# A two-stage Fourier transform beside attention, paired score matmuls and squares on GpSimd

## The chip, the cores and the metric

The kernel runs on one core of one Trainium2 chip. The metric is the device time of that core in microseconds (us); the time quoted for a kernel is the median of its runs.

The engines are called as in the profile: PE is TensorE (its weight loads are PEld), DVE is VectorE, ACT is ScalarE, POOL is GpSimd, SP is the engine that only issues DMA here. "L211" is line 211 of the kernel's source. An eviction is the copy of a matmul's result out of its PSUM tile (the memory that PE writes, here `ps`) into SBUF, the memory that the other work reads; ACT or DVE makes it.

## The reference

Attention without softmax makes `x` from `u`, `v` and `z`. Then `x` is projected three ways, the middle projection is convolved along the sequence with a filter by Fourier transforms, and two gates and an output projection follow. There are 8 batches, 3136 positions (64 times 49) and 256 channels; `z` has 64 channels.

```python
scores = z @ z.T / S                      # S = 3136
attn   = np.maximum(scores, 0.0) ** 2
x      = u * (attn @ v)

x1, x2, x3 = split(x @ w_proj)            # 3 x 256 channels
conv = irfft(rfft(x2) * rfft(filter_fft)) # along S
out  = (x1 * conv * x3) @ w_out
```

## The kernel before

It is two programs one after the other. The first does attention and the projections, and builds sine and cosine tables of 3136 by 1569 on the side; the second does the transform as matrix products with these tables, forward and back.

Attention, for a chunk of 512 queries and one block of 128 keys:

```python
ps = psA_sc.tile([P, CH], F32, name="ps_sc")
nc.tensor.matmul(ps[:krows, :cw], zT16[:, ds(kt * P, krows)], zT16[:, ds(s0, cw)], ...)   # L211, 64 rows
nc.scalar.activation(R[:krows, :cw], ps[:krows, :cw], AF.Relu)                            # L214
if kt % ACT_SQUARE_EVERY == (ACT_SQUARE_EVERY - 1):
    nc.scalar.activation(A16[...], R[...], AF.Square)
else:
    nc.vector.tensor_tensor(A16[...], R[...], R[...], ALU.mult)
for dh in range(2):
    nc.tensor.matmul(psout[:, dh, :cw], v16[:, kt, ds(dh * P, P)], A16[:, kt, :cw], ...)  # L222, 128 rows
```

The dense transform, forward (cosine and sine for every frequency block `ft`), then inverse:

```python
for t in range(NST):                                  # 25 blocks of positions
    for cN in range(NCH2):
        nc.tensor.matmul(pacc[:fw, 0, cN, :cwN], bandc[...], x2h[...], ...)     # L338
        nc.tensor.matmul(pacc[:fw, 1, cN, :cwN], bands[...], x2h[...], ...)     # L340
# ... product with the transformed filter, cut ...
for ft in range(NFT):                                 # 13 blocks of frequencies
    nc.tensor.matmul(po[:, :cw], Ac16[...], itC[...], start=(ft == 0), stop=False)   # L397
    nc.tensor.matmul(po[:, :cw], As16[...], itS[...], ...)                           # L399
```

Of the kernel before, what the change touches and what calls it, by code (L numbers as in the profile page):

```python
# [12 lines left out]
P = 128  # L13
# [6 lines left out]
CH = 512  # L20
ACT_SQUARE_EVERY = 4
# [3 lines left out]
def kernel(  # L25
# [14 lines left out]
    assert moe_w_proj.shape[1] == 3 * D and D == 2 * P and B % 2 == 0 and S % 4 == 0  # L40

    Fq = S // 2 + 1
    NST = ceil(S / P)
    NFT = ceil(Fq / P)
    NC = ceil(S / CH)

    def st_rows(t):
        return min(P, S - t * P)

    def ft_rows(t):  # L50
        return min(P, Fq - t * P)

    dram = ctx.enter_context(tc.tile_pool(name="dram_scratch", bufs=1, space=bass.MemoryType.DRAM))
    const = ctx.enter_context(tc.tile_pool(name="const", bufs=1))

    x2all = dram.tile([S, B * D], BF16, name="x2all")
    x1T_d = dram.tile([B * D, S], BF16, name="x1T_d")
    x3T_d = dram.tile([B * D, S], BF16, name="x3T_d")
    tabC = dram.tile([S, Fq], BF16, name="tabC")
    tabS = dram.tile([S, Fq], BF16, name="tabS")  # L60
    tabCi = dram.tile([Fq, S], BF16, name="tabCi")
    tabSi = dram.tile([Fq, S], BF16, name="tabSi")

    ident_f32 = const.tile([P, P], F32, name="ident_f32")
    make_identity(nc, ident_f32[:])
    ident_bf = const.tile([P, P], BF16, name="ident_bf")
    nc.vector.tensor_copy(ident_bf[:], ident_f32[:])
    negpi = const.tile([P, 1], F32, name="negpi")
    nc.vector.memset(negpi[:], -float(np.pi))

    wp16 = const.tile([P, 2, 3 * D], BF16, name="wp16")
# [4 lines left out]
    with ExitStack() as pha:  # L76
        tgencol = pha.enter_context(tc.tile_pool(name="tgencol", bufs=1))
        tgen = pha.enter_context(tc.tile_pool(name="tgen", bufs=2))
        batchp = pha.enter_context(tc.tile_pool(name="batchp", bufs=2))
        vpool = pha.enter_context(tc.tile_pool(name="vpool", bufs=2))  # L80
        batchin = pha.enter_context(tc.tile_pool(name="batchin", bufs=1))
        io = pha.enter_context(tc.tile_pool(name="io", bufs=2))
        achunk = pha.enter_context(tc.tile_pool(name="achunk", bufs=2))
        rring = pha.enter_context(tc.tile_pool(name="rring", bufs=4))
        ev = pha.enter_context(tc.tile_pool(name="ev", bufs=2))
        psA_pr = pha.enter_context(tc.tile_pool(name="psA_pr", bufs=2, space=bass.MemoryType.PSUM))
        psA_sc = pha.enter_context(tc.tile_pool(name="psA_sc", bufs=2, space=bass.MemoryType.PSUM))
        psA_out = pha.enter_context(tc.tile_pool(name="psA_out", bufs=1, space=bass.MemoryType.PSUM))
        tpsum = pha.enter_context(tc.tile_pool(name="tpsum", bufs=2, space=bass.MemoryType.PSUM))

        col_i = tgencol.tile([P, CH], I32, name="col_ramp_i")
        nc.gpsimd.iota(col_i[:], pattern=[[1, CH]], base=0, channel_multiplier=0)
        col_f = tgencol.tile([P, CH], F32, name="col_ramp_f")
        nc.vector.tensor_copy(col_f[:], col_i[:])
        pidx_i = tgencol.tile([P, 1], I32, name="pidx_i")
        nc.gpsimd.iota(pidx_i[:], pattern=[[0, 1]], base=0, channel_multiplier=1)
        pidx_f = tgencol.tile([P, 1], F32, name="pidx_f")
        nc.vector.tensor_copy(pidx_f[:], pidx_i[:])

        RND = float(1.5 * 2 ** 23)  # L100
        SHIFT_S = S // 2
        SHIFT_C = 3 * (S // 4)

        def table_gen_slices():
            for t in range(NST):
                rows = st_rows(t)

                def gen_band(t=t, rows=rows):
                    bandC = tgen.tile([P, Fq], BF16, name="bandC")
                    bandS = tgen.tile([P, Fq], BF16, name="bandS")  # L110
                    rowv = tgencol.tile([P, 1], F32, name="rowv")
                    nc.vector.tensor_single_scalar(rowv[:rows], pidx_f[:rows], float(t * P), ALU.add)
                    c0 = 0
                    while c0 < Fq:
                        w = min(CH, Fq - c0)
                        kf = tgencol.tile([P, CH], F32, name="kf")
                        if c0 == 0:
                            nc.vector.tensor_scalar(kf[:rows, :w], col_f[:rows, :w],
                                                    rowv[:rows, 0:1], None, ALU.mult)
                        else:  # L120
                            cf2 = tgencol.tile([P, CH], F32, name="cf2")
                            nc.vector.tensor_single_scalar(cf2[:rows, :w], col_f[:rows, :w], float(c0), ALU.add)
                            nc.vector.tensor_scalar(kf[:rows, :w], cf2[:rows, :w],
                                                    rowv[:rows, 0:1], None, ALU.mult)
                        t1 = tgencol.tile([P, CH], F32, name="t1")
                        nc.vector.tensor_scalar(t1[:rows, :w], kf[:rows, :w], 1.0 / S, RND, ALU.mult, ALU.add)
                        q0 = tgencol.tile([P, CH], F32, name="q0")
                        nc.vector.tensor_single_scalar(q0[:rows, :w], t1[:rows, :w], RND, ALU.subtract)
                        r = tgencol.tile([P, CH], F32, name="r")
                        nc.vector.scalar_tensor_tensor(r[:rows, :w], q0[:rows, :w], -float(S), kf[:rows, :w],  # L130
                                                       ALU.mult, ALU.add)
                        mneg = tgencol.tile([P, CH], F32, name="mneg")
                        nc.vector.tensor_single_scalar(mneg[:rows, :w], r[:rows, :w], 0.0, ALU.is_lt)
                        u1 = tgencol.tile([P, CH], F32, name="u1")
                        nc.vector.scalar_tensor_tensor(u1[:rows, :w], mneg[:rows, :w], float(S), r[:rows, :w],
                                                       ALU.mult, ALU.add)
                        for shift, band in ((SHIFT_S, bandS), (SHIFT_C, bandC)):
                            m2 = tgencol.tile([P, CH], F32, name="m2")
                            nc.vector.tensor_single_scalar(m2[:rows, :w], u1[:rows, :w], float(S - shift), ALU.is_ge)
                            up = tgencol.tile([P, CH], F32, name="up")  # L140
                            nc.vector.tensor_single_scalar(up[:rows, :w], u1[:rows, :w], float(shift), ALU.add)
                            uu = tgencol.tile([P, CH], F32, name="uu")
                            nc.vector.scalar_tensor_tensor(uu[:rows, :w], m2[:rows, :w], -float(S), up[:rows, :w],  # L143
                                                           ALU.mult, ALU.add)
                            nc.scalar.activation(band[:rows, ds(c0, w)], uu[:rows, :w], AF.Sin,
                                                 bias=negpi[:rows], scale=2.0 * np.pi / S)
                        c0 += w
                    nc.sync.dma_start(out=tabC[ds(t * P, rows), :], in_=bandC[:rows, :])
                    nc.sync.dma_start(out=tabS[ds(t * P, rows), :], in_=bandS[:rows, :])

                yield gen_band

        tslices = table_gen_slices()

        def emit_table_slices(n):
            for _ in range(n):
                fn = next(tslices, None)
                if fn is None:
                    return False
                fn()  # L160
            return True

        total_slices = NST
        slices_per_chunk = max(1, ceil(total_slices / max(1, B * NC)))

        inv_s2 = 1.0 / float(S) ** 2

        def batch_setup(b):
            zT16 = batchp.tile([dqk, S], BF16, name="zT16")
            uT16 = batchp.tile([P, 2, S], BF16, name="uT16")  # L170
            v16 = vpool.tile([P, NST, D], BF16, name="v16")
            NSTF = S // P
            zin = batchin.tile([P, NST, dqk], F32, name="zin")
# [23 lines left out]
        for b in range(B):  # L197
            zT16, uT16, v16 = setup
            if b + 1 < B:
                setup = batch_setup(b + 1)  # L200
# [249 lines left out]
```

## Time and profile before

| | |
|---|---|
| time, median of three runs | 3166.74 us |
| attention and projections | 0 to about 1620 us |
| dense transform | about 1620 to 3176 us |
| PE busy | 2727.0 us, 86% |
| GpSimd busy | 32.0 us, 1% |

The page of the profile starts with the busy time of each engine, then shows the span in 40 equal slices: each digit is the busy share in tenths, and PEclk is the clock that PE was granted, in tenths of full speed.

```profile
span 3175.6 us, 38107 instructions
PE 2727.0 (86%) x12632; PEld 1110.5 (35%) x12860; DVE 1634.2 (51%) x3711; ACT 1328.3 (42%) x3166; POOL 32.0 (1%) x51
...
PE   5876776876879898999995999999999588889999
...
PEclk9987877886889799999897999999999799899999
```

The busy times by stretch put numbers on the two halves. The columns are: the stretch, its length, busy time and instructions of PE, PEld, DVE, ACT and POOL, the granted clock, the DMA share and GB/s.

```profile
0.00:1620.00 1620.00, 1333.29 (x5313) 450.70 (x5410) 1221.78 (x2794) 1120.08 (x2554) 18.67 (x26) 0.87 0.24 64
1620.00:3176.00 1556.00, 1393.74 (x7321) 659.80 (x7450) 412.44 (x918) 208.19 (x614) 13.29 (x25) 0.96 0.41 107
```

In the second half PE is busy 1394 of 1556 us while DVE and ACT have little to do. In the first half three engines share the load and none is full.

The timeline of PE shows when runs of matmuls start (first column, us). Inside a run a 128x512 matmul starts every 0.215 us: three take 0.81 us and one alone takes about 0.38.

```profile
1573.82 0.81 PE L222 MATMUL psoutT<-A_16476,v_14198 128*128 128x512 bf16 x3
1574.56 0.39 PE L211 MATMUL ps_sc<-zT_14196 64*128 64x512 bf16 x1
1574.88 0.61 PE L222 MATMUL psoutT<-A_16476,v_14198 128*128 128x512 bf16 x2
```

From the score matmul (64 rows) to the next value matmul (128 rows) it is 0.32 us, not 0.215: about 0.1 us is lost at the change.

### The profile page before, as it was taken

To read this page: it belongs to the slowest core of one execution; us is meant where nothing else is said; L and a number is where in the kernel's file an instruction comes from. 1 tells how busy PE (TensorE), PEld (TensorE's weight loads), DVE (VectorE), ACT (ScalarE), POOL (GpSimd) and SP (SyncE) were. 2 spreads that over 40 slices of the span, in tenths; PEclk is the share of its full clock that TensorE was granted. 3 is DMA by queue.
4 is the path that set the end of the run, shared out by engine and by line. 5 is a ranking of instruction groups with operands and counts; after the bars stand their busy time and mean duration, and the time that the engine had idled before them with its cause. 6 is when DMAs were issued, how large, how long until landed. Compare 5 with 4: busy or idle time off the path is not lost.

```text
span 3175.6 us, 38107 instructions
## 1 busy us (share of the span) xinstructions
PE 2727.0 (86%) x12632; PEld 1110.5 (35%) x12860; DVE 1634.2 (51%) x3711; ACT 1328.3 (42%) x3166; POOL 32.0 (1%) x51
## 2 busy tenths in 40 slices
PE   5876776876879898999995999999999588889999
PEld 2323222222223233333332555553444233334444
DVE  5998998898985465666661434332111122231111
ACT  4866665765777576777771112120111000001111
POOL 0000000000000000000001000000000000000000
PEclk9987877886889799999897999999999799899999
DMA  7312312212212222121017434415452633334443
GB/s 153 101 46 53 100 41 62 91 46 67 90 44 43 80 52 71 35 48 32 30 39 173 107 90 97 108 45 175 124 161 82 159 64 61 62 78 133 151 130 82
DMA packets 456118, 270.55 MB, mean 85 GB/s; under 512 B 249430, under 2 KB 440238, under 8 KB 455920
## 3 DMA queue, kind: packets, MB, share of 16 engines
q1 hardware_dynamic: 268280, 175.17, 19.0%
q10 hardware_dynamic: 158216, 77.96, 9.5%
q0 software_dynamic: 29424, 14.98, 3.5%
q8 instruction: 100, 1.64, 0.2%
q14 instruction: 98, 0.80, 0.1%
HBM read 179.32 MB, written 103.59 MB: 89 GB/s over the span
## 4 chain that ended last, share of the span: by engine, by line
PE 70%; DVE 11%; DMA 10%; ACT 5%; issue 3%; SPq 0%; ACTq 0%; DVEq 0%
PE psoutT L222 17%; PE ps_sc L211 10%; PE psB_fwd L338 9%; PE psB_fwd L340 9%; PE psB_inv L397 8%; PE psB_inv L399 8%; ACT Rblk L214 3%; DMA uin<-in_u_dram 2%; DMA itS<-tabSi 2%; PE ps_pr L192 2%; DVE uu L143 2%; DMA x1T_d<-xiT 2%; PE ps_pr L234 2%; DMA bands<-tabS 2%; PE psB_tr L321 2%
## 5 line engine op out<-in xcount | busy, mean ns | idle before, releaser
L214 ACT ACTIVATE Rblk<-ps_sc 128x512 f32<-128x512 f32 (+2 forms) x1400 | 717.5, 542 | 209.4 <-PE ps_sc L211 174.3
L338 PE MATMUL psB_fwd<-x2h,bandc 128*128 128x512 bf16 (+2 forms) x1284 | 496.7, 387 | 68.8 <-DVE As_25282 L350 33.2
L340 PE MATMUL psB_fwd<-x2h,bands 128*128 128x512 bf16 (+2 forms) x1244 | 479.7, 386 | 0.7
L416 ACT ACTIVATE ostage<-psB_out 128x256 f32<-128x256 f32 (+1 forms) x200 | 76.6, 383 | 590.6 <-PE psB_out L414 404.1
L399 PE MATMUL psB_inv<-itS,As_25282 128*128 128x512 bf16 (+3 forms) x722 | 245.8, 357 | 3.3 <-DMA itS<-tabSi 1.7
L399 PE MATMUL psB_inv<-itS,As_17634 128*128 128x512 bf16 (+3 forms) x722 | 244.4, 355 | 1.8 <-issue 0.8
L397 PE MATMUL psB_inv<-itC,Ac_17633 128*128 128x512 bf16 (+2 forms) x706 | 238.9, 355 | 5.0 <-DMA itC<-tabCi 4.6
L397 PE MATMUL psB_inv<-itC,Ac_25281 128*128 128x512 bf16 (+2 forms) x706 | 240.3, 357 | 2.6 <-DMA itC<-tabCi 2.1
L338 PEld LDWEIGHTS <-bandc 128*128 128x128 bf16 (+2 forms) x1300 | 128.5, 99 | 157.0 <-issue 54.0
L340 PEld LDWEIGHTS <-bands 128*128 128x128 bf16 (+2 forms) x1300 | 128.6, 99 | 149.1 <-issue 40.5
L322 DVE COPY inv_st_c<-psB_tr 128x128 bf16<-128x128 bf16 (+2 forms) x190 | 42.0, 221 | 252.9 <-PE psB_tr L321 218.3
L350 DVE CAST As_25282<-psB_fwd 128x512 bf16<-128x512 f32 (+1 forms) x26 | 18.0, 691 | 279.2 <-ACT Ac_25281 L349 279.2
L349 ACT ACTIVATE Ac_25281<-psB_fwd 128x512 bf16<-128x512 f32 (+1 forms) x26 | 15.5, 596 | 349.3 <-PE psB_fwd L340 339.4
L192 PE MATMUL ps_pr<-ident_f_67,uin 128*128 128x128 f32 (+1 forms) x400 | 117.3, 318 | 40.1 <-DMA uin<-in_u_dram 10.9
L247 PE MATMUL ps_pr<-wp_76,xTch 128*128 128x256 bf16 (+1 forms) x400 | 78.1, 292 | 70.5 <-ACT xiT L238 55.4
L349 ACT ACTIVATE Ac_17633<-psB_fwd 128x512 bf16<-128x512 f32 (+1 forms) x26 | 15.5, 597 | 288.9 <-PE psB_fwd L340 288.2
L234 PE MATMUL ps_pr<-xTch,wp_76 128*128 128x512 bf16 (+1 forms) x430 | 117.2, 364 | 6.0 <-ACT xiT L238 1.7
L240 DVE CAST xiT<-ps_pr 128x512 bf16<-128x512 f32 (+1 forms) x112 | 69.7, 623 | 72.3 <-DMA x1T_d<-xiT 62.4
L321 PE MATMUL psB_tr<-ident_bf,bandc 128*128 128x128 bf16 (+3 forms) x325 | 71.2, 219 | 41.2 <-DMA bandc<-tabC 31.0
L397 PEld LDWEIGHTS <-Ac_25281 128*128 128x128 bf16 (+1 forms) x728 | 68.2, 98 | 90.8 <-issue 36.3
L250 ACT ACTIVATE x2blk<-ps_pr 128x256 bf16<-128x256 f32 (+1 forms) x200 | 75.6, 383 | 58.2 <-PE ps_pr L247 32.2
L397 PEld LDWEIGHTS <-Ac_17633 128*128 128x128 bf16 (+1 forms) x728 | 67.8, 98 | 88.0 <-issue 32.9
(1891 smaller groups left out, 4695.0 us busy)
## 6 DMA issues: line engine op xcount, KB each, us to landing
uin<-in_u_dram ACTq DMA_DIRECT2D x8, 3072.0 KB
out_dram<-ostage SPq DMA_DIRECT2D x192, 128.0 KB
bands<-tabS ACTq DMA_DIRECT2D x576, 32.0 KB
bandc<-tabC SPq DMA_DIRECT2D x576, 32.0 KB
itC<-tabCi SPq DMA_DIRECT2D x144, 128.0 KB
itS<-tabSi ACTq DMA_DIRECT2D x144, 128.0 KB
x1T_d<-xiT SPq DMA_DIRECT2D x96, 128.0 KB
x3T_d<-xiT SPq DMA_DIRECT2D x96, 128.0 KB
```

The costliest lines, as they stand in the source:

```text
L192: nc.tensor.transpose(ptu[:, :rows], uin[:rows, t, ds(dh * P, P)], ident_f32[:rows, :rows])
L211: nc.tensor.matmul(ps[:krows, :cw], zT16[:, ds(kt * P, krows)], zT16[:, ds(s0, cw)], start=True, stop=True)
L214: nc.scalar.activation(R[:krows, :cw], ps[:krows, :cw], AF.Relu)
L222: nc.tensor.matmul(psout[:, dh, :cw], v16[:, kt, ds(dh * P, P)], A16[:, kt, :cw], start=(kt == 0), stop=(kt == NST - 1))
L234: nc.tensor.matmul(pp[:, :cw], wp16[:, ksub, ds((comp * 2 + nb) * P, P)], xT[:, ksub, :cw], start=(ksub == 0), stop=(ksub == 1))
L247: nc.tensor.matmul(pp[:sw, :D], xT[:, ksub, ds(sb * P, sw)], wp16[:, ksub, D:2 * D], start=(ksub == 0), stop=(ksub == 1))
L321: nc.tensor.transpose(pti[:fw, :rows], src[:rows, t, :fw], ident_bf[:rows, :rows])
L338: nc.tensor.matmul(pacc[:fw, 0, cN, :cwN], bandc[:rows, t, :fw], x2h[:rows, t, ds(cN * CH, cwN)], start=(t == 0), stop=(t == NST - 1))
L340: nc.tensor.matmul(pacc[:fw, 1, cN, :cwN], bands[:rows, t, :fw], x2h[:rows, t, ds(cN * CH, cwN)], start=(t == 0), stop=(t == NST - 1))
L397: nc.tensor.matmul(po[:, :cw], Ac16[:fw, ft, ds(col0, P)], itC[:fw, ft, :cw], start=(ft == 0), stop=False)
L399: nc.tensor.matmul(po[:, :cw], As16[:fw, ft, ds(col0, P)], itS[:fw, ft, :cw], start=False, stop=(ft == NFT - 1))
L416: nc.scalar.activation(ost[:sw, sb, :], pp[:sw, :], AF.Copy)
```

## The change

Its intent is to shrink the transform and to hide it. It has four parts.

1. The 3136 points are split as 64 by 49, so that the transform is two small matrix products with a twiddle (a phase factor, here folded into a table) between them, forward and back. Two batches are packed as the real and imaginary part of one signal.
2. These stages are cut into small units and put between the attention steps of the next two batches. Only the last pair of batches is left for the end.
3. Score matmuls go in pairs: one block of keys from partitions 0-63, the next from 64-127, where a second copy of `z` stands. One wide eviction of up to 128x1024 serves both.
4. Squares go to ACT, DVE or GpSimd, whichever has the least estimated load; evictions go to ACT or DVE in the same way.

The diff does one thing more: `u` and `z` are loaded as bf16 and not as fp32, and so are transposed as bf16.

```diff
-ACT_SQUARE_EVERY = 4
+N1 = 64
+N2 = 49
+CHUNKS = (4, 4, 4, 3, 3, 3, 4)
+LAG = 3
...
+    def scores(b, c, i):
+        ps = ps_tile()                                   # one of three PSUM tiles [P, 2, 512]
+        for j in range(2):
+            hs = ds(N1 * j, N1)
+            nc.tensor.matmul(ps[:, j, :cw], zT[hs, ds((2 * i + j) * P, P)], zT[hs, ds(s0, cw)],
+                             start=True, stop=True)                                        # L465
... the last 64 keys, which have no partner, and the views Rv, pv and Av cut ...
+        R = rring.tile([P, 2, 512], F32, name="R")       # three buffers
+        if load.take(k * cw, ("act", "dve")) == "act":
+            nc.scalar.activation(Rv, pv, AF.Relu)                                          # L474
+        else:
+            nc.vector.tensor_single_scalar(Rv, pv, 0.0, ALU.max)                           # L476
+        eng = load.take(k * cw, ("act", "dve", "pool"))
+        if eng == "act":
+            nc.scalar.activation(Av, Rv, AF.Square)                                        # L481
+        else:
+            (nc.vector if eng == "dve" else nc.gpsimd).tensor_tensor(Av, Rv, Rv, ALU.mult) # L483
... values (L496), xT (L506), projections (L421, L447) and sine tables cut ...
+    def stage1(srcs, y, t0, n): ...      # 64-point transform, evicted to ye, stored to y_d
+    def stage2(p, kb): ...               # loads yl and hl; 49-point transform (L347); product tt (L351)
+    def stage3(p, kb): ...               # 49-point inverse (L360), evicted to ve, stored to v_d
+    def stage4(p, t0, n): ...            # loads vl and gl; 64-point inverse (L384), gates (L388)
+    def stage5(p, t0, n): ...            # output projection (L404), evicted to ot, stored (L411)
...
+        own += [lambda: proj1(b, c), lambda: proj3(b, c), lambda: proj2(b, c)]
+        own.insert(min(2, len(own)), lambda: (load_u(b1, c1), tr_u(b1, c1)))
... the units in `far` are spread between these and between the steps ...
```

## The prediction

> # Prediction
>
> **What bounds the kernel before.** The busy times by stretch show attention from 0 to about 1620 us, then the dense transform of 3136 points to 3176 us. In the second stretch PE is busy 1393 of 1556 us; the timeline shows 128x512 matmuls starting every 0.215 us, and the instruction order has 3.0 M moving columns there (1254 us at 0.42 ns a column): PE-bound. In the first, PE is busy 1334 of 1620 us at a granted clock of 0.78 to 0.95; ACT evicts every score tile (596 ns for 128x512), DVE squares three quarters (690 ns) and builds sine tables. The chain of waits puts 70% on PE.
>
> **PE after.** By the order of instructions, moving columns fall from 5.25 M to 2.76 M: the dense transform's 3.0 M become about 0.6 M, and attention stays. The paired scores (0.60 M columns) sit in partitions 0-63 and 64-127; the Trainium skill, "TensorE: Matmul & The Clock Gate", Part 3, says such row tiles run at the same time. No trace here shows it yet. If so, 0.30 M more go: about 1030 us at 0.42 ns. Changing between 64-row scores and 128-row values costs about 0.1 us each way (starts 0.31 to 0.33 us apart instead of 0.215 in the timeline near 1575 us); 728 steps instead of 1400 make it 146 us, not 280. Some 1000 matmuls of 128 columns add 30 us. PE sum: about 1200 us at full clock.
>
> **The other engines** (0.157 us + columns/0.96 on DVE, 0.17 us + columns/1.2 on ACT, fitted to 690 and 596 ns): DVE about 920 us (856 k columns, all-bf16 at double rate), ACT 840 us. GpSimd was 1% busy; now it squares 335 k columns. Estimate from the Trainium skill, "GPSIMD Engine Reference", 3.1 (4497 ns for 2048 fp32): 740 us, plus 245 DMA issues at 0.57 us (140 us), plus contention with DVE: 900 to 1150 us. No trace yet shows a GpSimd square. DMA falls from 270 to about 205 MB and is hidden.
>
> **Critical path.** The stages that ran alone (1556 us) now fill gaps beside attention, so nearly all their time is won, except the last pair of batches: 71 units alone at the end, through DRAM, about 115 us. Before attention starts: 25 us. In between, PE has 1155 us of work in order, but waits: three PSUM tiles carry 1304 uses, three R buffers feed GpSimd squares of over 2 us, the accumulator has one buffer. I take PE at 0.95 of its clock and 90% fed: 1155 / 0.855 = 1350 us. Sum, rounded down: 1450 us, ratio 0.46.
>
> **Predicted: 1450 us, 8 in 10 within 1290 to 1660.** Faster by over 2%: 0.98; within: 0.01; slower: 0.01.
>
> **What would show each step.** PE busiest, 80 to 90%; granted clock 0.9 or more until the last 115 us. Score matmuls of a pair starting within 0.05 us. GpSimd squares of 128x1024 near 2.3 us, its share 65 to 80%. DVE and ACT at 55 to 65%. PE's waits: mostly for R evictions (PSUM ring) and GpSimd's A tiles. A tail with PE under half busy.
>
> **What would make it wrong.** Row tiles that do not overlap (+126 us). GpSimd slower than 2.3 us or held up by DVE: it then sets the step, 1600 us or more. PE waits long enough to lower its clock. A DMA issue on GpSimd that waits for a buffer and holds the squares behind it. Better: if the waits overlap well, 1300 us.

## The result, and the profile after

The changed kernel takes 1449.7 us (median of four runs, 1446.39 to 1453.44), the one before 3165.3 us (a fourth run is added to the three above). The ratio is 0.4584, with a 95% interval of 0.4573 to 0.4594. All ratios here are the mean time of one kernel's runs over that of the other's in the same rounds, so not quite the ratio of the medians. To compare two experiments, the difference of their ratios is multiplied by the before time of about 3162 us.

The head of the page and its slices:

```profile
span 1451.7 us, 20110 instructions
PE 1245.9 (86%) x7379; PEld 562.1 (39%) x7379; DVE 960.5 (66%) x933; ACT 852.7 (59%) x953; POOL 800.7 (55%) x655
...
PE   3888999999988989999989999999999989985643
...
PEclk8999999999999999999999999999999999995566
```

PE is at eight tenths or more from slice 2 to slice 36. The busy times by stretch cut the run in three; 1297 us is just after the last attention matmuls.

```profile
0.00:40.00 40.00, 14.24 (x79) 6.99 (x80) 30.11 (x42) 17.48 (x15) 32.34 (x47) 0.81 0.72 116
40.00:1297.00 1257.00, 1157.42 (x6912) 514.66 (x6912) 881.25 (x850) 787.93 (x890) 768.35 (x609) 0.98 0.47 112
1297.00:1452.00 155.00, 74.29 (x393) 40.47 (x392) 49.16 (x43) 47.27 (x48) 0.00 (x0) 0.65 0.65 180
```

**The middle.** PE is busy 1157 of 1257 us, 92%, at a clock of 0.98. DVE stands at 70%, ACT at 63%, GpSimd at 61%.

**The start.** Scores begin at 11 us, but PE then waits twice for a square (the part in brackets is the idle time before the instruction, and who ended it).

```profile
20.34 4.80 PE L496 MATMUL psout<-A,vt 128*128 128x512 bf16 x12 [5.08 <-POOL A L483]
38.74 3.27 PE L496 MATMUL psout<-A,vt 128*128 128x512 bf16 x8 [10.66 <-DVE A L483]
```

The second wait is for a square on DVE, which is busy for all of the stretch from 20 to 40 us, mostly with the sine tables. Before its first instruction at 7.6 us PE waits for `z`.

**The waits of PE.** The view of waits (us in total, times, longest) has one large entry that lies in the middle:

```profile
PE ps L421 <- DVE xT L506: 70.0, 58, 5.2
PE ps L384 <- DMA vl<-v_d_73: 27.2, 7, 11.1
PE ps L347 <- DMA yl<-y_d_68: 24.3, 9, 8.6
...
PE psout L496 <- POOL A L483: 9.2, 9, 5.1
```

The 70 us are the first projection of each of the 56 chunks: it needs `xT`, which DVE makes from the accumulator that the chunk has just filled. GpSimd's squares cost PE only 9.2 us of waiting. The two entries with DMA belong to the end.

**The tail.** After 1297 us the last pair runs alone for 155 us, with PE busy for 74. The chain that ended last (start, length, what) shows evictions of `ye` that wait for the store before, loads of `yl` of near 5 us, and waits for `out` stores:

```profile
1303.04 1.92 DMA y_d_68<-ye
1305.07 1.03 ACT ye L108
1306.53 1.93 DMA y_d_68<-ye
...
1345.64 4.81 DMA yl<-y_d_68
...
1416.34 2.60 DMA out_dram<-ot
```

All of these DMAs go through SP's one queue. In its timeline twelve stores take 9.22 us to issue, and a load waits its turn behind them (single issues in the trace: eleven of 0.48 to 0.60 us and one of 1.97). In all, SP spends 79 of the tail's 155 us issuing.

```profile
1394.76 9.22 SPq L411 DMA_DIRECT2D out_dram<-ot  x12
1404.08 0.53 SPq L376 DMA_DIRECT2D gl<-g_d_63  x1
```

**The single operations.** The groups by shape give: line, engine, operation, out<-in, shapes, count, then busy us, mean ns of one, and the idle time before.

```profile
L483 POOL TENSOR_TENSOR A<-R 128x1024 bf16<-128x1024 f32 x142 | 282.9, 1996 | 182.6 <-ACT R L474 117.3 <-DVE R L476 64.3
...
L476 DVE TENSOR_SCALAR R<-ps 128x1024 f32<-128x1024 f32 x102 | 123.7, 1220 | 49.3 <-PE ps L465 45.3 <-POOL A L483 1.6 <-ACT R L474 1.1
...
L483 DVE TENSOR_TENSOR A<-R 128x1024 bf16<-128x1024 f32 x62 | 101.6, 1641 | 36.4 <-ACT R L474 36.3
...
L351 DVE TENSOR_TENSOR tt<-xs,hl 98x2048 bf16<-98x2048 bf16 x64 | 100.2, 1567 | 48.9 <-ACT xs L108 43.3 <-DMA hl<-h_d 4.9
```

A GpSimd square takes 1996 ns on average. On DVE the square takes 1641 ns, though an eviction from PSUM with as many columns takes 1220.

**The pairs.** The timeline of PE in the middle:

```profile
723.18 0.39 PE L465 MATMUL ps<-zT 64*128 64x512 bf16 x2
...
727.44 0.34 PE L465 MATMUL ps<-zT 64*128 64x384 bf16 x2
727.62 0.27 PE L312 MATMUL ps<-x_5232,T 64*128 64x256 bf16 x2
...
744.74 0.49 PE L496 MATMUL psout<-A,vt 128*128 128x384 bf16 x2
745.17 0.34 PE L465 MATMUL ps<-zT 64*128 64x384 bf16 x2
745.43 0.82 PE L496 MATMUL psout<-A,vt 128*128 128x384 bf16 x4
```

Two 128x384 scores take 0.34 us together, as much as one (mean 333 ns), while two 128x384 value matmuls take 0.49: the pair does run at the same time (its second matmul starts 3 ns after the first, median of all pairs). Where another 64-row matmul follows (L312), it starts 0.18 us after the pair. Where a 128-row matmul follows, it starts 0.26 us after.

### The profile page after: what moved, and what is told of

Its sections match the earlier page's. It is cut to its first block, busy times and chain, and to the rows that moved or that the text cites. A ratio compares the mean times of both kernels' runs of the same rounds, so it can differ in the third digit from the quotient of the medians.

```text
span 1451.7 us, 20110 instructions
## 1 busy us (share of the span) xinstructions
PE 1245.9 (86%) x7379; PEld 562.1 (39%) x7379; DVE 960.5 (66%) x933; ACT 852.7 (59%) x953; POOL 800.7 (55%) x655
## 2 busy tenths in 40 slices
DMA packets 164900, 173.69 MB, mean 120 GB/s; under 512 B 18496, under 2 KB 119040, under 8 KB 164800
## 5 line engine op out<-in xcount | busy, mean ns | idle before, releaser
L483 POOL TENSOR_TENSOR A<-R 128x768 bf16<-128x768 f32 (+3 forms) x398 | 663.4, 1673 | 426.9 <-ACT R L474 262.1
L496 PE MATMUL psout<-A,vt 128*128 128x512 bf16 (+3 forms) x2800 | 664.0, 359 | 25.2 <-DVE A L483 11.6
L474 ACT ACTIVATE R<-ps 128x1024 f32<-128x1024 f32 (+4 forms) x474 | 416.1, 886 | 275.7 <-PE ps L465 229.6
L496 PEld LDWEIGHTS <-vt 128*128 128x128 bf16 (+1 forms) x2800 | 251.3, 99 | 267.2 <-issue 97.6
L476 DVE TENSOR_SCALAR R<-ps 128x1024 f32<-128x1024 f32 (+3 forms) x254 | 264.7, 1048 | 125.4 <-PE ps L465 107.0
L465 PE MATMUL ps<-zT 64*128 64x512 bf16 (+2 forms) x1344 | 255.3, 360 | 4.0 <-ACT R L474 1.6
L483 DVE TENSOR_TENSOR A<-R 128x1024 bf16<-128x1024 f32 (+5 forms) x141 | 204.3, 1449 | 81.7 <-ACT R L474 81.4
L481 ACT ACTIVATE A<-R 128x1024 bf16<-128x1024 f32 (+4 forms) x189 | 177.8, 941 | 89.6 <-DVE R L476 87.0
L421 PE MATMUL ps<-xT,wp_142 128*128 128x512 bf16 (+2 forms) x448 | 118.1, 369 | 72.5 <-DVE xT L506 70.0
L351 DVE TENSOR_TENSOR tt<-xs,hl 98x2048 bf16<-98x2048 bf16 x64 | 100.2, 1567 | 48.9 <-ACT xs L108 43.3
L388 DVE TENSOR_TENSOR yT<-ps,gl 128x1024 bf16<-128x1024 f32 x48 | 58.7, 1222 | 57.4 <-DMA gl<-g_d_64 31.5
```

Source lines behind the costliest of these rows:

```text
L351: nc.vector.tensor_tensor(tt[:Q2], xs[:Q2].unsqueeze(1).to_broadcast([Q2, 2, KB * D]), hl[:Q2], ALU.mult)
L421: nc.tensor.matmul(ps[:, nb, :cw], wp16[:, ks, ds((2 * comp + nb) * P, P)], xT[:, ks, :cw], start=(ks == 0), stop=(ks == 1))
L465: nc.tensor.matmul(ps[:, j, :cw], zT[hs, ds((2 * i + j) * P, P)], zT[hs, ds(s0, cw)], start=True, stop=True)
L474: nc.scalar.activation(Rv, pv, AF.Relu)
L476: nc.vector.tensor_single_scalar(Rv, pv, 0.0, ALU.max)
L481: nc.scalar.activation(Av, Rv, AF.Square)
```

## The experiments

Two theories stood against each other. The first: in the middle PE sets the pace, so that PE's work and PE's waits count, and nothing else does. The rival: the eviction chain (three PSUM tiles, three R buffers, ACT, DVE and GpSimd) sets it. Ten variants of the changed kernel were built, then two that put together what helped.

A warning on correctness: every run was judged correct, but so was one that writes zeros on purpose (attention only, below). The largest value of the reference for the first batch is 2.9e-26, and the comparison does not tell that from zero. The variants are equivalent by construction; the comparison does not prove it.

| run | time, us | ratio to before | 95% interval |
|---|---|---|---|
| the change | 1449.7 | 0.4584 | 0.4573 to 0.4594 |
| one half | 1542.25 | 0.4876 | 0.4859 to 0.4893 |
| full rows | 1443.43 | 0.4564 | 0.4549 to 0.4579 |
| bursts | 1801.54 | 0.5693 | 0.5674 to 0.5713 |
| attention only | 1098.96 | 0.3472 | 0.3458 to 0.3485 |
| no GpSimd squares | 1431.0 | 0.4520 | 0.4506 to 0.4534 |
| tail queue | 1440.15 | 0.4547 | 0.4533 to 0.4560 |
| tail pools | 1434.83 | 0.4531 | 0.4521 to 0.4540 |
| tail both | 1417.3 | 0.4478 | 0.4467 to 0.4488 |
| u transposes first | 1404.87 | 0.4448 | 0.4436 to 0.4460 |
| groups of two | 1457.48 | 0.4625 | 0.4608 to 0.4642 |
| best, pairs | 1352.8 | 0.4279 | 0.4261 to 0.4297 |
| best, full rows | 1353.02 | 0.4281 | 0.4263 to 0.4299 |

### Are the pairs worth what they should be?

```diff
-                hs = ds(N1 * j, N1)
+                hs = ds(0, N1)
```

> Both score blocks of a pair are taken from partitions 0-63 (z is held twice, so the result is the same); the order of instructions on every engine stays the same. Theory (PE sets the pace between 45 and 1297 us, and the two halves of a pair run at the same time): 0.30 M columns at 0.42 ns come back, about +126 us, 1550 to 1600 us. Rival (the eviction of scores by ACT, DVE and GpSimd sets the pace): under +40 us.

Measured: 1542.25 us; 0.4876 - 0.4584 is 0.0292, or 92 us. In the timeline a pair of 128x512 now takes 0.60 us where it took 0.39, and PE's busy time grew from 1245.9 to 1370.5 us:

```profile
PE 1370.5 (89%) x7317; PEld 583.9 (38%) x7379; DVE 944.1 (61%) x933; ACT 857.2 (56%) x953; POOL 793.6 (51%) x655
...
750.13 0.60 PE L465 MATMUL ps<-zT 64*128 64x512 bf16 x2
750.66 0.82 PE L421 MATMUL ps<-xT,wp 128*128 128x512 bf16 x3
```

The 125 us of work came back as estimated, and 92 us of it reached the time, which is just below the 1550 to 1600 us expected; the rest filled waits (PE's wait for `xT` fell from 70.0 to 42.2 us). That PE sets most of the pace is shown, and the rival's bound of 40 us is broken. But the pairs look better here than they are, as the next run shows.

```diff
-                hs = ds(N1 * j, N1)
+                hs = ds(0, P)
...
-    inv_s2 = 1.0 / float(S) ** 2
+    inv_s2 = 0.25 / float(S) ** 2
```

> Each score matmul contracts over all 128 partitions, where z stands twice: the score is doubled and the scale of the result divided by four. No pair runs at the same time, but no matmul uses 64 rows in attention either. Same order of instructions. Theory (each change between 64 and 128 rows costs PE about 0.1 us, 146 us in all): 1575 - 146, about 1430 us, within 25 us. Rival (the 0.1 us is not from the row mode): as one_half, about 1575 us.

Measured: 1443.43 us. Its interval overlaps that of the change, so the two are not told apart; it is 99 us faster than one half, with the same order of instructions. Its timeline has no gap at the change of operation:

```profile
745.03 0.82 PE L496 MATMUL psout<-A,vt 128*128 128x384 bf16 x4
745.69 0.49 PE L465 MATMUL ps<-zT 128*128 128x384 bf16 x2
746.02 0.60 PE L347 MATMUL ps<-yl,FT 98*98 98x512 bf16 x2
```

Four value matmuls of 384 columns take 0.66 us to the next start, 0.165 each, and two scores take 0.33. By the traces, PE changes between up to 64 and more rows 1418 times with one half and 280 times with full rows, so the 99 us are about 0.09 us a change. So the change between 64 and 128 rows costs what the timelines said, about 0.1 us each way, and this eats the whole gain of running a pair at once. Pairing by row halves is worth nothing here against scores over all 128 rows.

```diff
-    for gi in range(len(steps) + LAG):
-        scores of step gi; units; values of step gi - LAG          (LAG = 3)
+    for g2 in range(0, len(steps) + LAG, 2):
+        scores of steps g2, g2+1; units; values of the two steps LAG before   (LAG = 4)
```

> Scores are put out for two steps at a time, then the values of two steps: by the order of instructions the changes between 64-row and 128-row matmuls fall from 1464 to 822. Theory (each costs PE about 0.1 us and PE sets the pace): -64 us, 1370 to 1410. Rival (two score tiles at once take two of the three PSUM tiles and their evictions then come in bursts): 1450 or more.

Measured: 1457.48 us, 0.4625, which is 13 us slower by the ratios. PE's busy time fell from 1245.9 to 1219.6 us, so part of the saving is there, but PE waits more: its idle time rose from 206 to 233 us, though its wait for `xT` fell from 70.0 to 41.2. Waits of scores for an R eviction, 1.6 us on ACT in the change, are now:

```profile
PE ps L465 <- ACT R L474: 14.9, 22, 1.6
...
PE ps L465 <- DVE R L476: 7.3, 10, 3.0
```

This fits the rival's bursts on the three PSUM tiles, but the named waits do not add up to what was lost, and LAG and the place of the units changed with the order, so the exact cause is open. If the bursts are the cause, PE sets the pace only as long as the evictions can follow.

### What is the place of the transform worth?

```diff
             queue_filter()
+            while far:
+                far.popleft()()
...
             queue_pair(far_pending.pop())
+            while far:
+                near.append(far.popleft())
+            while near:
+                near.popleft()()
```

> The transform of the filter and of each pair of batches is put out in one burst as soon as its data exist, not beside the attention of the next two batches. Theory (beside attention a pair costs only its PE work, some 50 us; alone it costs what the last pair costs at the end, 155 us): three pairs and the filter, about +350 us less what the edges overlap, 1650 to 1800 us. Rival (the gain is the smaller transform, not its place): under 1520 us.

Measured: 1801.54 us, 0.1109 or 351 us above the change: the size expected before overlap of the edges, and just above the range. The slices show the bursts as dips of PE, and of its granted clock:

```profile
PE   4468989976558999985657898995755899997653
...
PEclk7659999985569999996568999997566999998556
```

PE's busy time for the same work grew from 1245.9 to 1362.3 us, at a mean granted clock of 0.838 instead of 0.939; the other 234 us are added idle time. So about 350 us of the whole gain come from where the same units stand.

```diff
-        if k == 0:
-            queue_filter()
...
-            queue_pair(far_pending.pop())
+            far_pending.pop()
...
+                nc.sync.dma_start(out=out[b]..., in_=zero[:])     # zeros, on purpose
```

> No transform and no output projection: attention, projections and tables stay; the output is zeros on purpose (wrong result). Theory (PE-bound, so the transform's PE work of about 200 us is paid for even beside attention, and 155 us of tail go): 1450 - 155 - 165, about 1130 us, 1090 to 1170. Rival (the transform only fills idle gaps of PE): about 1295 us, the tail alone gone.

Measured: 1098.96 us. The transform with the output projection therefore costs 1449.7 - 1099.0, about 351 us, also when it is spread. Of these 155 us are the tail; the other 196 us are paid in the middle. PE busy falls by 251 us to 994.9:

```profile
PE 994.9 (91%) x5594; PEld 412.2 (37%) x5648; DVE 755.7 (69%) x775; ACT 678.5 (62%) x764; POOL 682.2 (62%) x580
```

Taking away the tail's 74 us of PE work leaves 177 us, close to the 196: work placed beside attention is not free, it costs its PE time. The rival's 1295 us is out.

This also divides the gain. Before, the stretch of attention took about 1620 us and that of the transform 1545 (3165 - 1620). After, they take 1099 and 351. About 1195 us of the gain come from the transform and about 520 from attention. How the 520 us divide over wider evictions, fewer changes of row mode, bf16 transposes, the smaller tables and the higher clock was not tested.

### What do the squares on GpSimd bring?

```diff
-        eng = load.take(k * cw, ("act", "dve", "pool"))
+        eng = load.take(k * cw, ("act", "dve"))
```

> All squares go to ACT and DVE, none to GpSimd. The 398 GpSimd squares are worth about 0.9 us each on ACT or DVE, some 360 us over both, so DVE and ACT rise to about 1040 us each, below PE's 1246. Theory (PE sets the pace): 1450 to 1530 us. Rival (without the GpSimd squares ACT and DVE would set it): over 1560 us. And if GpSimd and DVE hold each other up: DVE squares of 128x1024 fall from a mean of 1641 to about 1220 ns and the product tt of 98x2048 from 1567 to about 1230 ns; if not, both stay.

Measured: 1431.0 us, faster than the change by 0.0064 or 20 us, with intervals clear of each other. Neither theory expected that. DVE and ACT rose to 1044.8 and 1020.3 us as estimated. The groups of DVE:

```profile
L483 DVE TENSOR_TENSOR A<-R 128x1024 bf16<-128x1024 f32 x128 | 155.0, 1221 | 53.5 <-ACT R L474 52.7
L476 DVE TENSOR_SCALAR R<-ps 128x1024 f32<-128x1024 f32 x97 | 117.4, 1220 | 26.1 <-PE ps L465 24.6 <-ACT A L481 0.7
...
L351 DVE TENSOR_TENSOR tt<-xs,hl 98x2048 bf16<-98x2048 bf16 x64 | 78.2, 1223 | 43.4 <-ACT xs L108 39.2 <-DMA hl<-h_d 3.2
```

The square fell from 1641 to 1221 ns and the product `tt` from 1567 to 1223, while the eviction from PSUM stayed at 1220. So GpSimd's squares slowed those operations of DVE that read two tensors from SBUF, and none of those compared that read PSUM. A few with one SBUF input were slower too: the eight copies of `z` at L135 took 573 ns in the change and 180 here. In the change's trace the 40 squares of 128x1024 and products `tt` with no GpSimd square beside them take 1222 ns on average, and the 56 that started during one 2028. GpSimd pays too, but less: half of its 128x1024 squares take 1892 ns or less, and 20 of 142 take over 2000, up to 3457. The Trainium skill, "Advanced Engine Details and Errata", GPSIMD Details, says that GpSimd shares a read and a write interface with DVE and conflicts with DVE instructions in a 2-port perf mode or with two SBUF inputs; for two SBUF inputs these runs agree, with the numbers above. With ACT and DVE at 71% and 73%, PE did not need the help. A GpSimd square takes 1996 ns against 1221 on DVE, so its R buffer should be held longer; what that is worth is not shown. Some 5 us of the 20 are at the start: PE was busy 19.3 us of the first 40 instead of 14.2. Most of the rest is shorter waits in the middle, where PE's idle time fell from 100 to 88 us; no single entry shows them.

### What binds the tail?

The first variant only moves the last pair's loads from SP's queue to GpSimd's, which is idle then.

```diff
-        nc.sync.dma_start(out=hl[:Q2], in_=h_d[:, kb])
+        (nc.gpsimd if p == NP - 1 else nc.sync).dma_start(out=hl[:Q2], in_=h_d[:, kb])
... the same for yl, vl and gl ...
```

> Only the last pair of batches: its loads are issued by GpSimd (idle then), its stores stay with SP. Theory (the tail of about 155 us is bound by one in-order DMA queue: 0.4 to 0.8 us an issue, and loads behind stores that wait): stages 2 to 5 shorten, about -40 us, 1400 to 1425 us. Rival (the tail is bound by what DMA moves, or by too few buffers): within 12 us of 1450.

Measured: 1440.15 us, 12 us better by the ratios: at the edge of what the rival gave, and far from the 40 of the theory.

The second only gives the last pair's DMA tiles the buffers that attention no longer needs.

```diff
-        ye = yev.tile([P, 2, 2, D], BF16, name="ye")
+        ye = (aring.tile([P, 2, 2, D], BF16, tag="A", name="ye") if y is y_d[NP - 1]
+              else yev.tile([P, 2, 2, D], BF16, name="ye"))
... yl and vl from vpool, hl from rring, ve and gl from aring ...
```

> Only the last pair: its DMA tiles take the buffers that attention no longer needs (9 for loads, 6 for stores, 3 for h, instead of 2 or 3); queues as before. Theory of too few buffers: about -40 us. Theory of the one queue: only stage 1 gains (its evictions wait 1.9 us each for the store before), -10 to -20 us, 1430 to 1440.

Measured: 1434.83 us, 17 us better: what the theory of the one queue gave, and not the 40 of too few buffers. The third has both.

> Both changes of the tail together. If queue and buffers bind one after the other: more than the sum of the two, about -65 us, 1375 to 1400 us. If DMA bandwidth binds: no better than the better of the two.

Measured: 1417.3 us, 0.0106 or 34 us better. The two apart gave 29; the difference of 5 is within the noise of these ratios (about 7), and the sum is half of what was hoped. The tail, from 1294 us on, is now 121 us, with the DMA share at 0.80 and 235 GB/s instead of 0.65 and 180:

```profile
1294.00:1415.00 121.00, 61.94 (x392) 37.48 (x388) 48.66 (x43) 46.40 (x48) 51.32 (x80) 0.74 0.80 235
```

So queue and buffers each bound a part and their gains add; that they bind one after the other, with more than the sum to win, is not shown. What remains is nearer to what DMA moves, which no run tested. The Trainium skill, "DMA: Bandwidth & Descriptors", Rules for kernel authors, says that spreading DMAs over issuing engines gives no bandwidth and saves only issue time. The queue alone fits that: 12 us, where SP's issues in the tail of the change take 0.31 to 0.62 us each, by the means of the kinds of load and store.

### What is the wait for xT worth?

```diff
-            own.insert(min(2, len(own)), lambda: (load_u(b1, c1), tr_u(b1, c1)))
+            own.insert(0, lambda: (load_u(b1, c1), tr_u(b1, c1)))
```

> At each of the 56 chunk borders the transposes of u come before the first projection, which needs xT from DVE. Theory (PE is the pace and waits some 70 us in all for xT at the borders, the longest wait of its matmuls): the transposes and a transform unit fill part of it, -25 to -45 us, 1405 to 1425. Rival (the wait only moves to the next chunk's values, which need the one accumulator free): within 10 us of 1450.

Measured: 1404.87 us, 0.0136 or 43 us better, from one changed number. The waits of PE:

```profile
PE psout L496 <- DVE xT L506: 18.1, 25, 1.7
...
PE ps L421 <- DVE xT L506: 4.5, 9, 1.2
```

Of 70.0 us at the projection 4.5 are left; a part moved to the next chunk's values, which wait for the one accumulator: from 4.1 to 18.1 us. The sum fell by 51.5 us, and the time by 43. A wait of PE in the middle is worth nearly its length.

### Together

> What helped by itself, together: no squares on GpSimd (-19 us), both changes of the tail (-33 us), transposes of u first at the chunk borders (-45 us); scores stay in pairs of 64 rows. If the gains add (they lie in different waits): about 1353 us, 1340 to 1370. If DVE and ACT, now fuller by 80 and 170 us, hold up the border: over 1375 us.

> The same, with scores over all 128 rows instead of pairs of 64 (-6 us by itself): about 1347 us, and not slower than best_pairs. If pairing is worth something once other waits are gone: slower than best_pairs by more than 5 us.

Measured: 1352.8 us and 1353.02 us. The gains add as expected. Pairs and full rows are equal, with intervals that all but coincide, so that pairing is worth nothing here either. Both beat the change by 97 us. PE is busy 91% of the span, and 95% between 200 and 1200 us (953 us).

```profile
span 1350.5 us, 19807 instructions
PE 1222.4 (91%) x7379; PEld 563.8 (42%) x7379; DVE 1045.1 (77%) x1120; ACT 1017.4 (75%) x1164; POOL 191.2 (14%) x340
```

## Why the prediction was right or wrong

The time was right, 1450 against 1449.7 us, but no one should admire the last digit. The terms were 25 + 1350 + 115, which is 1490; the text rounded this down to 1450. Measured they are 40 + 1257 + 155, which is 1452 of the profiled run. The middle was 93 us too long, the start 15 and the tail 40 too short. Errors of opposite sign, and a rounding, made the hit; the mechanism made the range.

- **PE sets the pace: right.** PE was the busiest engine at 86%; adding 125 us of PE work cost 92 us, removing about 177 us of it from the middle gave back 196, and removing about 51 us of its waits gave 43.
- **PE's work of about 1155 us in the middle: right** (1157 us busy, with ends that are modelled). What failed is the factor 0.855: its parts were a clock of 0.95 (measured 0.98) and 90% fed. Busy over length is 92%, with the clock's effect already in it.
- **Pairs run at the same time: right**, as the Trainium skill, "TensorE: Matmul & The Clock Gate", Part 3, says: 0.39 us for two 128x512, and 0.60 us when both use the same half. The prediction counted this gain (126 us) and the cost of row changes (146 us) as two items and did not see that they belong to one choice. Full rows show that they cancel.
- **Changes of row mode, 0.1 us each: right**, seen as gaps in timelines before and after, and as 99 us between one half and full rows. Those runs differ only in the rows of the score matmuls and a constant of the scale.
- **The transform fills gaps, "nearly all their time is won": right in size, loose in words.** It costs 351 us in place of about 1545, of which 196 us are paid beside attention, because PE has few gaps to fill.
- **The tail: right in kind, too small.** 155 us instead of 115; PE was busy 48% of it, as "under half" said. The prediction called DMA hidden; in the tail it is not. The 115 us left out the issue times of SP's one queue and the few buffers. Mending both gave 34 us of the 40 that were missed.
- **The start: about right in lost time, other cause.** PE is idle for 26 of the first 40 us, but most of it not before attention: PE waits 7.6 us for `z`, scores start at 11 us, and then PE waits for squares while DVE builds tables.
- **GpSimd: wrong in size and in role.** The square took 1996 ns, not 2.3 us, and GpSimd was busy 801 us, 55%, not 900 to 1150 us and 65 to 80%. The contention was put on GpSimd's account; what the runs show is mostly DVE slowed, its square by a third (1641 against 1221 ns) and its product by 28%. PE hardly waited for GpSimd (9.2 us), and without its squares the kernel is 20 us faster.
- **Where PE waits: wrong.** Named were R evictions and GpSimd's tiles; the largest wait was for `xT` at the chunk borders, 70 us. The prediction did list the single accumulator, next to the true place, but gave it no number.
- **DVE at 920 us and ACT at 840: near**, 960.5 and 852.7. The excess on DVE is no more than the contention: an estimate from the two shapes above is 62 x 0.42 + 64 x 0.34, about 48 us, and all shapes of squares with `tt` give about 75, so the work without contention was forecast somewhat too high. DMA moved 173.69 MB, not 205.

## What to carry to other kernels

When one engine sets the pace, work placed beside it still costs its full time on that engine: count it, and count every wait of that engine, since the cheapest 43 us here came from reordering two operations. Running two half-height matmuls at once, and using an idle engine, are trades with a price elsewhere (a change of row mode, a shared port), and only a run with and without them shows the balance. A predicted total that fits proves little until its terms are compared one by one.

## What the Trainium skill lacked or had wrong

- "TensorEngine Tiling (Array Packing)", Key Properties, says that a change of tiling mode drains TensorE, without a figure. Here it costs about 0.10 us for each change between 64 and 128 rows (a start 0.26 us after a pair of 384 columns in place of 0.16), with 1464 changes by the order of instructions and 1418 counted in the trace. The page's speedup for row tiling does not set this against the gain; here they cancel (1352.8 us with pairs, 1353.02 us with full rows).
- "GPSIMD Engine Reference", 3.1, gives 4497 ns for a `tensor_tensor` of 2048 fp32 columns. A square of 1024 columns with bf16 output took 1996 ns here on average (median 1892), somewhat less than half of that.
- The same page and "Advanced Engine Details and Errata" say that GpSimd and DVE conflict when DVE has two SBUF inputs, without a figure of what this costs a kernel. Here DVE paid most: 1641 against 1221 ns for a square, and 1567 against 1223 ns for a product of bf16. A DVE eviction from PSUM was unchanged at 1220 ns. GpSimd's own squares had a mean of 1996 ns at a median of 1892.
